# Every pair of f tiles goes by Strassen's scheme, with the sums of g's blocks made on GpSimd

## The chip, the cores and the metric

The kernel runs on one core of one Trainium2 chip. The metric is the device time of one execution in microseconds, and less is better. One core has five engines with instruction queues of their own: TensorE (PE in the profile, with its weight loads as PEld), VectorE (DVE), ScalarE (ACT), GpSimd (POOL) and SyncE (SP, which here issues transfers only). Each engine takes its instructions strictly in the order in which the program put them there, and waits on semaphores for the others.

## The reference

For each of 8 batches and 8 heads, 32 packed queries attend over 576 keys, and then the 576 queries attend over the 32 packed results. The heads are joined to a matrix of 4608 tokens by 512, and that goes through two matrix products with an ELU between.

```
def sm_attn(qq, kk, vv):
    a = softmax(scale * qq @ kk.T)          # with the maximum taken off, eps 1e-9
    return a @ vv
p_packed = sm_attn(p, k, v)                 # 8 x 8 x 32 x 64
x = sm_attn(q, p_packed, p_packed)          # 8 x 8 x 576 x 64 -> 4608 x 512
h = x @ w_in                                # 512 x 2048
g = where(h > 0, h, exp(min(h, 0)) - 1)
out = g @ w_out                             # 2048 x 512
```

## The kernel before, in words

**What is computed.** The first product is folded into the attention. `ppT` holds the packed results of a batch, `m` is `ppT` times `w_in` (the "m steps", line 838, four to a batch), and `h` is the second softmax `a` times `m`. Numbers are split into a rounded part and a remainder (`a_hi`, `a_lo`, `m_hi`, `m_lo`, and two parts of `g` and of the output weights `wo_a`, `wo_b`), so each product is three matmuls: high by high, high by low, low by high.

**Tiles.** The 2048 columns of `h` are 16 "f tiles" of 128. A batch's 576 tokens are two windows (`win` 0 and 1). One window has 256 tokens, the other 320, of which 64 are kept aside in `hb` and stored in DRAM (`rest_dram`); four batches' leftovers make a window of 256 at the end (`rest`, called batches 8 and 9 here). Batches 0, 1 and window (2, 0) go f tile by f tile (lines 1342 to 1455), with the weights still being converted on VectorE and ScalarE.

**Strassen's scheme.** From window (2, 1) on, f tiles go in pairs (`strassen_pair`, with `u` the pair's number, 8 pairs to a window). The 256 tokens by 256 columns of `g` are four blocks of 128 by 128, in a buffer `w8` (two of these; the leftovers' windows use a `kvq` buffer instead). For a Strassen pair three instructions (`sums`, line 1155) make four further blocks. ScalarE then casts seven blocks into `g` (`hi`), VectorE subtracts for the remainders (`lo`, line 1164), and TensorE makes seven products of three matmuls with 256 columns each: 21 matmuls on line 1229. The weights of these products are the stored blocks and four sums of them, `sw`, made once on VectorE (`strassen_weights`), written to DRAM (`sw_dram`), and fetched again for every Strassen pair: four loads of 256 KB (line 1187) into a ring of eight `sw` buffers. A pair that `S_PLAINS` names goes "plain" instead: no sums, four blocks in `hi` and `lo`, no `sw` loads, and either 12 matmuls of 512 columns (windows whose list has pair 0) or 6 of 512 and 12 of 256. `S_PLAINS` names 17 of the 88 pairs of batches 2 to 7.

**What sets the order.** Nothing is left to a runtime scheduler. The program collects operations with `op(prio, {engine: cost}, fn, deps, take, use, ...)`; `take` and `use` name buffers of rings (`R`: three `g`, two `w8`, eight `sw`, eight PSUM banks). `schedule()` then plays them through with these costs, `SWITCH` for every change of TensorE between full tiles and the small tiles (64 rows by 32 columns) of attention and m steps, lags and priorities, and writes each engine's queue in the order that comes out. The costs decide the order only; on the chip every wait is a semaphore.

**The ends.** At the start, `warm_up` runs `N_WARM` matmuls on a constant, and then TensorE follows batch 0's attention as its data comes. At the end, the last window and the second leftover window finish together (`both`); VectorE adds four accumulators in PSUM to `part` (`add1` to `add5`, line 1260), and SyncE stores two halves of it (line 1302).

Of the kernel before, what the change touches and what calls it, by code (L numbers as in the profile page):

```python
# [22 lines left out]
def packed_attention_elu_ffn(  # L23
# [63 lines left out]
    SPARE = 0.75  # L87
    HOLD = 2.1500000000000004
# [10 lines left out]
    SWITCH = 0.105  # L99
    N_WARM = 14  # L100
    F_PLAIN = 0
# [5 lines left out]
        (2, 0): [1, 2],  # L107
        (2, 1): [0],
        (3, 0): [1],
        (3, 1): [0, 2, 5],  # L110
        (4, 0): [0, 5],
        (4, 1): [1],
        (5, 0): [2, 7],
        (5, 1): [0, 4],
        (6, 0): [6],
        (6, 1): [1, 5, 6, 7],
# [38 lines left out]
    class Banks:  # L155
# [3 lines left out]
        def places(self, bufs, now):  # L159
            free = [h is None or h.released(now) for h in self.held]  # L160
            out = []
            for b in bufs:
                at = [i for i in range(0, len(free), b.n) if all(free[i:i + b.n])]
# [16 lines left out]
    class Buf:  # L180
        def __init__(self, ring, make, n=1):
            self.ring, self.make, self.n, self.users, self.t = ring, make, n, [], None
            self.free = False
# [7 lines left out]

    ops = []
# [3 lines left out]
    def op(prio, on, fn, deps=(), take=(), use=(), after=(), mode=None, lag=0):  # L196
        o = Op()
        o.lag = lag
# [8 lines left out]
    def schedule():  # L207
# [9 lines left out]
        idle_at = {e: 0.0 for e in GAP}  # L217
# [4 lines left out]
        def engine_for(o):  # L222
# [8 lines left out]
            e = min(o.on, key=lambda e: max(idle_at[e], now) + o.on[e] + spare * (e == "DVE"))  # L231
            return e if idle_at[e] <= now else None

        while todo:
            held = {}
            for n, o in enumerate(todo[:400]):
                if o.wait:
                    continue
                if o.ready > now:
                    if o.ready <= now + HOLD and o.prio < HOLD_K and len(o.on) == 1:  # L240
                        held.setdefault(*o.on, o)
                    continue
# [16 lines left out]
                idle_at[e] = now + cost + GAP[e]  # L259
                o.start, o.end = now, now + cost + LAG[e] + o.lag  # L260
# [94 lines left out]
    def warm_up(e):  # L355

        x = part_sb[:, 0, :E // 2].bitcast(BF16)
        for _ in range(N_WARM):
            nc.tensor.matmul(warm_b.t, lhsT=x[:, :P], rhs=x, start=True, stop=True)

    warm_b = banks(1)
    op(-1000, {"PE": 1.2 + 0.31 * N_WARM}, warm_up, take=[warm_b])
# [83 lines left out]
    def attention(b, ts):  # L446
# [182 lines left out]
        if b < S_FIRST[0] + 1:  # L629
            o1 = op(t, {"PE": 1.15}, s1, ld_k, take=ps1 + e1s, use=[p_b] + k_b, after=[free], mode=1)  # L630
# [6 lines left out]
        else:  # L637
            kept, o1 = [], None
            for half in range(2):
                ps = ps1[half]  # L640
                o1 = op(
                    t, {"PE": 0.52}, lambda e, half=half, ps=ps: s1_half(e, half, ps), ld_k,
# [56 lines left out]
        o = op(ts[2], {"PE": 1.36}, pv, ld_v + tr_done, take=[ps, pp_b], use=v_b + e1T, mode=2)  # L699
        done = []  # L700
        for g in range(G):
            def norm(e, g=g, ps=ps):
# [9 lines left out]
                ts[2], {"ACT": 0.31, "DVE": 0.27}, norm, [o, o5] + done,  # L712
# [15 lines left out]
        prev = []  # L728
        for half in range(2):
            ps = banks(2)  # L730
            t1, t2 = temp(), st.af if whole else temp()
# [12 lines left out]
            def fold(e, g, ps=ps, t1=t1):  # L744
                nc.vector.transpose(out=flat(t1)[:, g * HS:(g + 1) * HS], in_=ps.t[:, g, :HS])
# [46 lines left out]
            def lo(e, cs=cs, done=done):  # L792
# [6 lines left out]
            o = op(t, {"PE": 0.52}, s2, [lds["q"][half % len(q_b)], st.ppT_op],  # L799
                   take=[ps, t1], use=[q_b[half % len(q_b)], st.ppT], mode=1)  # L800
            f0 = op(t, {"DVE": 0.44}, lambda e, fold=fold: fold(e, 0), [o] + prev, use=[ps, t1])
            f1 = op(t, {"DVE": 0.44}, lambda e, fold=fold: fold(e, 1), [f0], use=[ps, t1])
# [21 lines left out]
    def mstep(b, c, part, parts_, prio, deps=()):  # L824
# [25 lines left out]
        def lo(e):  # L850
# [7 lines left out]
        if part:  # L858
            pre.append(st.m_done[c, part - 1])
        o = op(prio, {"PE": 1.0 / parts_ + 0.03}, mm, pre, take=[ps] + (m_b if part == 0 else []),  # L860
               use=[st.ppT] + (m_b if part else []), mode=1)
# [5 lines left out]
        if not whole:  # L867
            st.m_done[c, part] = op(
                prio, {"DVE": 1.2 if parts_ == 1 else 0.68}, lo, [h], use=[ps] + m_b
            )  # L870
        st.m_parts = parts_

# [46 lines left out]
    for b in range(B):  # L919
        for c in range(NFC):  # L920
# [3 lines left out]
            else:  # L924
                t = TMS[b] if b in TMS else TM
                mstep(b, c, 0, 1, first_use["b", b] - NS + t[c])
# [115 lines left out]
    def strassen_pair(i, b, win, f):  # L1042
# [103 lines left out]
        def sums(e):  # L1146
# [3 lines left out]
            for out, x, y, o in (  # L1150
# [3 lines left out]
            ):  # L1154
                nc.vector.tensor_tensor(out=out, in0=x, in1=y, op=o)  # L1155
# [17 lines left out]
        if not plain:  # L1173
            done = [op(i + 1, {"DVE": 1.08}, sums, done, use=[w8])]
# [26 lines left out]
        if f == 0:  # L1201
            accs[mine] = [banks(1) for _ in range(3)] + [accs["rest"][3] if both else banks(1)]
        acc = accs[mine]
# [49 lines left out]
        if last:  # L1253
# [38 lines left out]
            y = op(q, {"DVE": 0.69}, add4, [y, acc[2].last], use=[part, acc[2]])  # L1292
            y = op(q, {"DVE": 0.42 if both or rest else 0.69}, add5, [y, acc[3].last], use=[part, acc[3]])
# [6 lines left out]
            def store(e):  # L1300
                for r in range(2):
                    nc.sync.dma_start(
# [3 lines left out]
            op(q, {"DMA": 1.4}, store, [y], use=[part])  # L1306

    acc = None
    for i, (b, win, f) in enumerate(order):
# [119 lines left out]
        if first:  # L1429
            acc = [banks(1) for _ in range(n_t)]  # L1430

# [130 lines left out]
```

## Time and profile before

| what | value |
|---|---|
| median of 3 runs | 665.98 us (664.81 to 666.00) |
| the profiled execution | 665.54 us, of which 663.7 us are the span from first to last instruction |
| TensorE busy | 642.7 us (97%), 5963 matmuls |
| VectorE busy | 562.7 us (85%), 1270 instructions |
| ScalarE busy | 429.5 us (65%) |
| GpSimd busy | 19.4 us (3%), 27 instructions |
| moved from HBM | 124.25 MB read, 27.26 MB written |

Rows name a line of the kernel, an engine, an operation, and out<-in by the program's tile names. "Idle before" is time in which the engine had nothing running just ahead of these instructions, and behind it stands who ended that wait. Times inside the trace are in microseconds from the span's start. Matmuls overlap in the array, so their durations don't add up; what counts is the time from one's start to the next one's.

### The profile page before, as it was taken

To read this page: it belongs to the slowest core of one execution; us is meant where nothing else is said; L and a number is where in the kernel's file an instruction comes from. 1 tells how busy PE (TensorE), PEld (TensorE's weight loads), DVE (VectorE), ACT (ScalarE), POOL (GpSimd) and SP (SyncE) were. 2 spreads that over 40 slices of the span, in tenths; PEclk is the share of its full clock that TensorE was granted. 3 is DMA by queue.
4 is the path that set the end of the run, shared out by engine and by line. 5 is a ranking of instruction groups with operands and counts; after the bars stand their busy time and mean duration, and the time that the engine had idled before them with its cause. 6 is when DMAs were issued, how large, how long until landed. Compare 5 with 4: busy or idle time off the path is not lost.

```text
span 663.7 us, 15743 instructions
## 1 busy us (share of the span) xinstructions
PE 642.7 (97%) x5963; PEld 563.8 (85%) x5963; DVE 562.7 (85%) x1270; ACT 429.5 (65%) x863; POOL 19.4 (3%) x27
## 2 busy tenths in 40 slices
PE   6599999999999999999999999999999999999996
PEld 3277788898779898997889998998889988999996
DVE  2899889999995799978986998769999978878785
ACT  4599898777664567875575567675676566555451
POOL 0000101222110000000000000000000000000000
PEclk9699999999999999999999999999999999999999
DMA  8795973899951367888658887886589764785863
GB/s 339 297 316 173 298 244 80 202 211 263 320 195 27 116 215 247 261 260 265 231 173 290 289 253 243 283 259 235 163 283 319 240 199 123 222 229 186 284 227 132
DMA packets 94443, 152.55 MB, mean 230 GB/s; under 512 B 25248, under 2 KB 34464, under 8 KB 94112
## 3 DMA queue, kind: packets, MB, share of 16 engines
q1 hardware_dynamic: 91488, 146.30, 67.2%
q0 software_dynamic: 2880, 5.24, 5.3%
q8 instruction: 47, 0.77, 0.4%
q14 instruction: 28, 0.23, 0.1%
HBM read 124.25 MB, written 27.26 MB: 228 GB/s over the span
## 4 chain that ended last, share of the span: by engine, by line
PE 85%; ACT 6%; DMA 5%; DVE 2%; issue 1%; SPq 1%; POOL 0%; DVEq 0%; ACTq 0%; POOLq 0%
PE psum L1229 37%; PE psum L1073 20%; PE psum L1342 6%; PE psum L838 4%; PE psum L1452 4%; PE psum L1455 4%; PE psum L1453 4%; ACT tops L352 2%; DMA out<-part 2%; PE psum L737 1%; PE psum L692 1%; DMA raw<-in_w_out 1%; DMA kvq<-in_qT 1%; PE psum L596 1%; PE psum L666 1%
## 5 line engine op out<-in xcount | busy, mean ns | idle before, releaser
L1229 PE MATMUL psum<-sw,g 128*128 128x256 f32 x1044 | 150.4, 276 | 0.2 <-DMA sw<-sw_dram 0.2
L1229 PEld LDWEIGHTS psum<-sw,g 128*128 128x128 f32 x1044 | 133.0, 192 | 5.0 <-issue 3.5
L1164 DVE TENSOR_TENSOR g<-w,g 128x896 fp32r<-128x896 f32 (+1 forms) x88 | 88.4, 1006 | 21.1 <-ACT g L352 20.8
L1073 PE MATMUL psum<-a_hi,m_hi 128*128 128x320 f32 (+1 forms) x352 | 103.2, 293 | 0.1
L1073 PE MATMUL psum<-a_lo,m_hi 128*128 128x320 f32 (+1 forms) x352 | 101.4, 288 | 0.0
L1073 PE MATMUL psum<-a_hi,m_lo 128*128 128x320 f32 (+1 forms) x352 | 101.4, 288 | 0.0
L352 ACT CAST g<-w 128x896 fp32r<-128x896 f32 (+1 forms) x88 | 77.1, 876 | 35.6 <-PE psum L1229 16.3
L1229 PE MATMUL psum<-wo_a,g 128*128 128x256 f32 (+1 forms) x519 | 83.5, 293 | 0.0
L1229 PE MATMUL psum<-wo_b,g 128*128 128x256 f32 (+1 forms) x522 | 82.9, 290 | 0.0
L1229 PEld LDWEIGHTS psum<-wo_a,g 128*128 128x128 f32 x519 | 71.5, 191 | 5.2 <-issue 3.0
L1229 PEld LDWEIGHTS psum<-wo_b,g 128*128 128x128 f32 x522 | 70.8, 191 | 5.9 <-issue 3.5
L1155 DVE TENSOR_TENSOR w<-w 128x128 f32<-128x128 f32 (+1 forms) x213 | 70.8, 333 | 5.2
L1073 PEld LDWEIGHTS psum<-a_hi,m_hi 128*128 128x128 f32 x352 | 67.1, 191 | 7.5 <-issue 1.8
L1085 ACT ACTIVATE e<-psum 128x320 f32<-128x320 f32 x96 | 41.7, 434 | 40.4 <-PE psum L1073 37.0
L1073 PEld LDWEIGHTS psum<-a_lo,m_hi 128*128 128x128 f32 x352 | 67.2, 191 | 0.5
L1073 PEld LDWEIGHTS psum<-a_hi,m_lo 128*128 128x128 f32 x352 | 67.0, 190 | 0.0
L1085 ACT ACTIVATE w<-psum 128x512 f32<-128x512 f32 x40 | 23.8, 597 | 36.5 <-PE psum L1073 16.9
L1088 ACT ACTIVATE e<-e 128x320 f32<-128x320 f32 x96 | 45.1, 471 | 2.4
L1080 DVE SCALAR_TENSOR_TENSOR w<-e,psum 128x256 f32<-128x256 f32 x96 | 39.7, 414 | 8.1 <-ACT e L1088 7.9
L1360 ACT ACTIVATE e<-psum 128x256 f32<-128x256 f32 (+1 forms) x80 | 32.6, 407 | 21.5 <-PE psum L1342 17.4
L1369 DVE SCALAR_TENSOR_TENSOR e<-e,psum 128x256 f32<-128x256 f32 x80 | 33.0, 414 | 10.8 <-ACT e L1366 10.6
L838 PE MATMUL psum<-w_in_sb,ppT 64*32 64x512 f32 (+1 forms) x640 | 35.5, 518 | 6.0 <-DVE w_in_sb L397 5.8
(124 smaller groups left out, 1237.8 us busy)
## 6 DMA issues: line engine op xcount, KB each, us to landing
sw<-sw_dram SPq DMA_DIRECT2D x284, 256.0 KB, 3.9
kvq<-in_v SPq DMA_DIRECT2D x16, 512.0 KB, 5.4
out<-part SPq DMA_DIRECT2D x32, 256.0 KB, 3.6
sw_dram<-sw SPq DMA_DIRECT2D x32, 256.0 KB, 4.1
raw<-in_w_in SPq DMA_DIRECT2D x16, 511.8 KB, 4.5
raw<-in_w_out SPq DMA_DIRECT2D x16, 511.8 KB, 5.3
kvq<-in_kT SPq DMA_DIRECT2D x14, 576.0 KB, 5.1
kvq<-in_qT SPq DMA_DIRECT2D x14, 576.0 KB, 5.6
```

The lines of the kernel that those rows point to most:

```text
L352: (nc.scalar.copy if e == "ACT" else nc.vector.tensor_copy)(out=out, in_=in_)
L838: nc.tensor.matmul(ps.t[cols_of(pair), g, :w], lhsT=st.ppT.t[rows_of(g), pair, :], rhs=w_in_sb[rows_of(g), pair, c * FC + part * w:c * FC ...
L1073: nc.tensor.matmul(ps, lhsT=m_b[p].t[:, g, o:o + P], rhs=in_turn(st.a.t[q][:, g, cols]), start=(n == 0), stop=(n == 3 * G - 1),)
L1080: nc.vector.scalar_tensor_tensor(out=out, in0=e_, scalar=-1.0, in1=ps, op0=ALU.add, op1=ALU.max)
L1085: nc.scalar.activation(out=out, in_=ps, func=AF.Relu, scale=-1.0)
L1088: nc.scalar.activation(out=x, in_=x, func=AF.Exp, scale=-1.0)
L1155: nc.vector.tensor_tensor(out=out, in0=x, in1=y, op=o)
L1164: nc.vector.tensor_tensor(out=g_b.all[:, 7 * P:(7 + b1 - b0) * P], in0=blocks(b0, b1), in1=g_b.all[:, :(b1 - b0) * P].bitcast(F32), op=ALU ...
L1229: nc.tensor.matmul(a.t[:, at * H:(at + rhs.shape[1]) * H], lhsT=operand(blk, p), rhs=rhs, start=new and n == k == 0, stop=a.final == (u, m ...
L1342: nc.tensor.matmul(ps_b.t[:, :n_tok], lhsT=m_b[x].t[:, g, o:o + P], rhs=in_turn(st.a.t[y][:, g, cols]), start=(n == 0), stop=(n == 3 * G - 1),
L1360: nc.scalar.activation(out=pairs(e_b.t[:, :n_tok]), in_=h(slice(0, n_tok)), func=AF.Relu, scale=-1.0)
L1369: nc.vector.scalar_tensor_tensor(out=pairs(out), in0=pairs(e_b.t[:, cs]), scalar=-1.0, in1=h(cs), op0=ALU.add, op1=ALU.max,)
```

## The change

The three sums of a Strassen pair are issued to GpSimd in place of VectorE, as three operations with costs of their own, and `S_PLAINS` is empty, so all 88 pairs go by the scheme. The planner gets a resource "port": of the operations in `TWO`, one on VectorE and one on GpSimd are not placed at the same time. Several other costs and rules change with it: a higher `SWITCH`, m steps that follow each other in order, softmax folds of 2 x 288 columns in one VectorE instruction in place of two, banks limited for some accumulators, 20 fillers of two matmuls each at the start, and the last two stores placed apart. `M_PAIR`, `S1_FULL` and `S2_BOTH` are empty lists, so what hangs on them isn't reached.

```
-    SWITCH = 0.105
+    SWITCH = 0.2
     N_WARM = 14
+    N_FILL = 20
     S_PLAINS = {
-        (2, 1): [0],
...                               (17 pairs in all of windows (2, 1) to (6, 1), and 2 of (2, 0))
     }
+    TWO = {"top", "join", "high", "low", "ssub", "smul", "hi", "lo", "sub_own", "cast", "sums", "words", "t13", "t24"}
+            if o.two and e in ("DVE", "POOL") and idle_at["port"] > now:
+                return None
+    for _ in range(N_FILL):
+        warm_op = op(-30, {"PE": 0.44}, lambda e: warm_up(e, 2), after=[warm_op], use=[warm_b], lag=-0.2)
-            def fold(e, g, ps=ps, t1=t1):
-                nc.vector.transpose(out=flat(t1)[:, g * HS:(g + 1) * HS], in_=ps.t[:, g, :HS])
+            def fold(e, ps=ps, t1=t1):
+                nc.vector.transpose(
+                    out=flat(t1).rearrange("p (g s) -> p g s", g=G), in_=ps.t[:, :, :HS]
+                )
-        def sums(e):
+        def sums(e, at):
...
-                nc.vector.tensor_tensor(out=out, in0=x, in1=y, op=o)
+            nc.gpsimd.tensor_tensor(out=out, in0=x, in1=y, op=o)
-            done = [op(i + 1, {"DVE": 1.08}, sums, done, use=[w8])]
+            for n, cost in enumerate((0.41, 0.69, 0.41)):
+                done = [op(i + 1, {"POOL": cost}, lambda e, n=n: sums(e, n), done, use=[w8], lag=0.05 - LAG["POOL"], two=True)]
-            op(q, {"DMA": 1.4}, store, [y], use=[part])
+            if both:
+                op(q, {"DMA": 0.7}, lambda e: store(e, (1,)), [y4], use=[part])
+                op(q, {"DMA": 0.7}, lambda e: store(e, (0,)), [y], use=[part])
+            else:
+                op(q, {"DMA": 1.4}, store, [y], use=[part])
```

TensorE's queue at a pair that was plain, the third of window (3, 1), before (line 1073 is `h`, line 1229 the output products):

```order
L1073 MATMUL psum<-a_lo,m_hi 128x256
L1073 MATMUL psum<-a_hi,m_lo 128x256
L1229 MATMUL psum<-wo_a,g 128x512 x12
L1073 MATMUL psum<-a_hi,m_hi 128x256
L1073 MATMUL psum<-a_lo,m_hi 128x256
```

The same pair on TensorE after (line 1122 is `h`, 1281 the output products, 862 an m step):

```order
L1122 MATMUL psum<-a_lo,m_hi 128x256
L1122 MATMUL psum<-a_hi,m_lo 128x256
L1281 MATMUL psum<-wo_a,g 128x256 x3
L1281 MATMUL psum<-sw,g 128x256 x9
L1281 MATMUL psum<-wo_a,g 128x256 x6
L862 MATMUL psum<-w_in_sb,ppT 32x512 x8
L1281 MATMUL psum<-sw,g 128x256 x3
L1122 MATMUL psum<-a_hi,m_hi 128x256
```

Twelve matmuls of 512 columns became 21 of 256, twelve of which read `sw`. VectorE's queue in window (3, 0) before, where 1080 is the ELU's last step, 1155 the sums and 1164 the remainders (`w_3681` is a `w8` buffer):

```order
L1080 SCALAR_TENSOR_TENSOR w_3681<-e,psum 128x256
L1080 SCALAR_TENSOR_TENSOR hb<-e,psum 128x64
L1155 TENSOR_TENSOR w_3681<-w_3681 128x128
L1155 TENSOR_TENSOR w_3681<-w_3681 128x256
L1155 TENSOR_TENSOR w_3681<-w_3681 128x128
L1080 SCALAR_TENSOR_TENSOR w_3732<-e,psum 128x256
L1080 SCALAR_TENSOR_TENSOR hb<-e,psum 128x64
L1164 TENSOR_TENSOR g<-w_3681,g 128x896
```

VectorE's queue in that window after, with 1129 for the ELU and 1213 for the remainders:

```order
L1129 SCALAR_TENSOR_TENSOR w_3727<-e,psum 128x256
L1129 SCALAR_TENSOR_TENSOR hb<-e,psum 128x64
L1129 SCALAR_TENSOR_TENSOR w_3792<-e,psum 128x256
L1129 SCALAR_TENSOR_TENSOR hb<-e,psum 128x64
L1213 TENSOR_TENSOR g<-w_3727,g 128x896
```

The three sums are gone from between the ELU and the remainders; GpSimd's queue holds three of them for each pair instead, behind its 20 stores of the first batches. TensorE's queue at the start, after batch 0's product with `v`, before (718 and 737 are batch 0's second attention, 838 the first m step, 1335 the first `h`):

```order
L692 MATMUL psum<-kvq,tmp 32x64 x40
L718 MATMUL psum<-ident,pp 128x128
L737 MATMUL psum<-q_181,ppT 32x288 x16
L838 MATMUL psum<-w_in_sb,ppT 32x256 x8
L1335 MATMUL psum<-k_292,m_hi 128x256 x4
```

The same place after, where line 361 is a filler:

```order
L698 MATMUL psum<-kvq,tmp 32x64 x40
L361 LDWEIGHTS part
L361 MATMUL psum<-part 128x512
L361 LDWEIGHTS part
L361 MATMUL psum<-part 128x512
L724 MATMUL psum<-ident,pp 128x128
```

Fillers stand between the steps of batch 0's attention: 2 of the 40 matmuls ahead of its first product, 8 and 6 around its transposes, 2 here, 4 behind line 724 and 18 between the two halves of line 747, which was 737.

More of the change, by code (lines that the diff above doesn't have):

```diff
@@ L162, in places @@
             for b in bufs:
-                at = [i for i in range(0, len(free), b.n) if all(free[i:i + b.n])]
+                at = [i for i in range(0, min(len(free), b.lim), b.n) if all(free[i:i + b.n])]
                 if not at:
@@ L239, in schedule @@
                 if o.ready > now:
-                    if o.ready <= now + HOLD and o.prio < HOLD_K and len(o.on) == 1:
-                        held.setdefault(*o.on, o)
+                    if o.ready <= now + HOLD and o.prio < HOLD_K:
+                        for e in o.on:
+                            held.setdefault(e, o)
                     continue
@@ L259, in schedule @@
                 idle_at[e] = now + cost + GAP[e]
+                if o.two and e in ("DVE", "POOL"):
+                    idle_at["port"] = idle_at[e]
                 o.start, o.end = now, now + cost + LAG[e] + o.lag
@@ L727, in attention @@
         st.a_done, st.af_done = [], []
-        prev = []
+        prev, s2s = [], []
         for half in range(2):
-            ps = banks(2)
-            t1, t2 = temp(), st.af if whole else temp()
+            if half and b in S2_BOTH:
+                ps, t1 = second
+                t2 = temp()
+            else:
+                ps = banks(2)
+                t1, t2 = temp(), st.af if whole else temp()
             mx, sm = {}, {}
@@ L798, in attention @@
             t = ts[4 + half]
[L799 to L802, printed above, removed]
+            if b in S2_BOTH:
+                s2s.append((s2, ps, t1))
+                if half == 0:
+                    ps1_, t11 = banks(2), temp()
+                    second = ps1_, t11
+                    o2 = op(
+                        t, {"PE": 0.97}, lambda e: [x[0](e) for x in s2s], [lds["q"][0], lds["q"][1], st.ppT_op],
+                        take=[ps, ps1_, t1, t11], use=q_b + [st.ppT], mode=1,
+                    )
+                o = o2
+            else:
+                o = op(t, {"PE": 0.485}, s2, [lds["q"][half % len(q_b)], st.ppT_op],
+                       take=[ps, t1], use=[q_b[half % len(q_b)], st.ppT], mode=1)
+            f1 = op(t, {"DVE": 0.77}, fold, [o] + prev, use=[ps, t1])
             o = op(t, {"DVE": 0.75}, smax, [f1], use=[t1])
@@ L859, in mstep, with mstep_pair, mstep_done, done @@
             pre.append(st.m_done[c, part - 1])
-        o = op(prio, {"PE": 1.0 / parts_ + 0.03}, mm, pre, take=[ps] + (m_b if part == 0 else []),
-               use=[st.ppT] + (m_b if part else []), mode=1)
+        if also:
+            return ps, m_b, mm, pre, hi, lo_, whole
+        ready = mstep_done(b, c, part, parts_, prio, ps, m_b, hi, lo_, whole)
+        ready(op(prio, {"PE": 0.86 / parts_}, mm, pre, after=[b >= NB0 and m_last[0] or None],
+                 take=[ps] + (m_b if part == 0 else []), use=[st.ppT] + (m_b if part else []), mode=1))
+    def mstep_pair(b, c, prio):
+        st = sts[b]
+        both = [mstep(b, c + n, 0, 1, prio, also=True) for n in range(2)]
+        o = op(
+            prio, {"PE": 0.86 * 2}, lambda e: [x[2](e) for x in both], both[0][3] + both[1][3],
+            take=[x[0] for x in both] + both[0][1] + both[1][1], use=[st.ppT], after=[m_last[0]], mode=1,
+        )
+        for n, (ps, m_b, _, _, hi, lo_, whole) in enumerate(both):
+            mstep_done(b, c + n, 0, 1, prio, ps, m_b, hi, lo_, whole)(o)
+    def mstep_done(b, c, part, parts_, prio, ps, m_b, hi, lo_, whole):
+      st = sts[b]
+      def done(o):
+        m_last[0] = o
         h = op(
```

69 lines of the change are left out of this document (39 added, 30 removed).

## The prediction

> **What bounds the kernel now.** I read the page's totals and slices first, then TensorE's waits, then the chain that ended last. In these lines the slices show where TensorE is not full, and the chain which engine sets the end.
>
> ```profile
> span 663.7 us, 15743 instructions
> PE 642.7 (97%) x5963; PEld 563.8 (85%) x5963; DVE 562.7 (85%) x1270; ACT 429.5 (65%) x863; POOL 19.4 (3%) x27
> PE   6599999999999999999999999999999999999996
> PE 85%; ACT 6%; DMA 5%; DVE 2%; issue 1%; SPq 1%; POOL 0%; DVEq 0%; ACTq 0%; POOLq 0%
> ```
>
> TensorE is full but for the first slice and the last. Its waits say the same; each row has the total, how often, and the longest.
>
> ```profile
> PE psum L838 <- DVE w_in_sb L397: 5.8, 1, 5.8
> PE psum L666 <- ACT tmp L579: 2.9, 3, 2.1
> ...
> PE psum L1229 <- DMA sw<-sw_dram: 0.2, 1, 0.2
> ```
>
> The large ones lie in the first 37 us; the products of Strassen's scheme waited once, for 0.2 us. So VectorE at 85% is busy but in nobody's way, and taking sums from it gives nothing by itself. The time can only change by what TensorE has to stream, by waits that are new, and at the two ends. I make the sum against the profiled execution's 665.5 us, which lies 0.4 below the median of 665.98.
>
> **Plain pairs become Strassen pairs.** Here the chain has a plain pair (12 matmuls) and a Strassen pair (21) each in one piece; the other two rows count the 512-column matmuls that go.
>
> ```profile
> 318.88 2.59 PE psum L1229 x12
> ...
> 322.81 2.35 PE psum L1229 x21
> ...
> L1229 PE MATMUL psum<-wo_a,g 128*128 128x512 f32 x84 | 20.1, 381 | 0.0
> ...
> L1229 PE MATMUL psum<-wo_b,g 128*128 128x512 f32 x66 | 15.8, 381 | 0.0
> ```
>
> 2.59/12 is 0.216 us for 512 columns, 2.35/21 is 0.112 for 256. A plain pair of the first kind saves 2.59 - 2.35 = 0.24; of the second kind (6 wide, 12 narrow) 6 x 0.216 + 12 x 0.112 - 2.35 = 0.29. The 150 wide matmuls are 8 pairs of 12 and 9 of 6, so 8 x 0.24 + 9 x 0.29 = **-4.5 us**, all of it on the path.
>
> **Changes between full and small tiles.** TensorE's order after has 61 stretches of small tiles (attention, m steps) where it had 58. What a stretch costs beyond its columns:
>
> ```profile
> 262.47 0.83 PE L1229 MATMUL psum<-wo_b,g 128*128 128x256 f32 x6
> 263.23 1.09 PE L838 MATMUL psum<-w_in_sb,ppT 64*32 64x512 f32 x16
> 264.25 0.40 PE L1073 MATMUL psum<-a_hi,m_hi 128*128 128x320 f32 x1
> 264.49 0.30 PE L1073 MATMUL psum<-a_lo,m_hi 128*128 128x320 f32 x1
> ...
> 185.29 1.88 PE psum L838 x32
> ```
>
> Six narrow matmuls take 0.76 to the next start instead of 0.67 (0.09 going in); the first one behind takes 0.24, where the next of its kind takes 0.14 (0.10 coming out); one m step is 1.02 and two in a row 1.88, so 0.16 is paid once a stretch. Together 0.35, and three more are **+1.05 us**. The rest of TensorE's matmuls are the same in number and shape, fillers aside.
>
> **The start.** TensorE waited 5.8 us ahead of the first m step and then ran at a slow clock. Windows give engines' busy time, then the granted clock, DMA share and GB/s; then come TensorE's first products of `h`, and what VectorE waited for.
>
> ```profile
> 15.00:20.00 5.00, 2.12 (x33) 0.69 (x33) 3.12 (x7) 1.18 (x3) 0.00 (x0) 0.60 1.03 404
> 20.00:25.00 5.00, 1.11 (x16) 0.23 (x16) 4.86 (x10) 2.26 (x5) 0.00 (x0) 0.50 0.56 227
> 25.00:30.00 5.00, 4.85 (x32) 3.07 (x40) 3.23 (x7) 3.08 (x8) 0.00 (x0) 0.53 0.96 378
> ...
> 25.15 3.78 PE L1335 MATMUL psum<-k,m_hi 128*128 128x256 f32 x8 [0.74 <-ACT m_hi L352]
> 31.64 1.13 PE L1335 MATMUL psum<-k,m_hi 128*128 128x256 f32 x4 [0.77 <-ACT m_hi L352]
> ...
> 28.12 0.42 DVE L1369 SCALAR_TENSOR_TENSOR e<-e,psum 128x256 f32<-128x256 f32 x1 [0.97 <-ACT e L1366]
> 29.95 0.75 DVE L765 TENSOR_REDUCE sm<-tmp 128x18 f32<-128x576 f32 x1 [0.81 <-ACT tmp L761]
> ```
>
> At clock 0.5 eight rows took 3.78 us; at 1.00 four took 1.13, so eight would take about 2. The 18 fillers between the halves of line 737 occupy 18 x 0.216 = 3.9 of the 5.8 us that were idle, and should hold the clock. TensorE then finishes those products some 1.8 us sooner, but VectorE, behind ScalarE, can make up only the 0.97 + 0.81 = 1.8 us that it idled. Against it stand two fillers more ahead of batch 0's first product (0.4), of which I count half as late at the first m step. I take **-1.2 us**, between -1.8 (nothing late) and +0.4 (the clock falls anyway and the delay stays).
>
> **The end.**
>
> ```profile
> 658.61 1.34 DVE L1260 TENSOR_TENSOR part<-part,psum 128x256 f32<-128x256 f32 x3
> 659.98 0.84 SPq L1302 DMA_DIRECT2D out<-part  x2
> ```
>
> One of the last two stores now needs only `add4` and is issued during `add5`; the other's issue moves up by half of 0.84, **-0.4 us** (0 if both land together as before).
>
> **The sums on GpSimd.** They leave VectorE and add nothing to TensorE; their price is how much later `hi`, `lo` and the products come. The first two rows are the sums now, then `lo` of a Strassen pair and of a plain one, then all that GpSimd does here on 128 columns.
>
> ```profile
> L1155 DVE TENSOR_TENSOR w<-w 128x128 f32<-128x128 f32 x142 | 40.7, 286 | 2.8
> L1155 DVE TENSOR_TENSOR w<-w 128x256 f32<-128x256 f32 x71 | 30.2, 425 | 2.5
> ...
> L1164 DVE TENSOR_TENSOR g<-w,g 128x896 fp32r<-128x896 f32 x71 | 76.8, 1083 | 16.3 <-ACT g L352 16.1
> L1164 DVE TENSOR_TENSOR g<-w,g 128x512 fp32r<-128x512 f32 x17 | 11.6, 685 | 4.8 <-ACT g L352 4.7
> ...
> masks.py:199 POOL TENSOR_SCALAR_AFFINE_SELECT ident<-ident 128x128 f32<-128x128 f32 x1 | 0.3, 286 | 0.0
> masks.py:197 POOL MEMSET ident<- 128x128 f32 x1 | 0.2, 205 | 0.3 <-POOLq L1551 0.3
> ```
>
> On VectorE a pair's sums are 2 x 0.29 + 0.43 = 1.0 us. No row has a two-input instruction on GpSimd. From below: one input read and written took 286 ns, as on VectorE, so 1.0 again. From above: a write alone took 205; two reads and a write one after the other would be 0.6, and for three instructions with four blocks some 2.4. I take 1.5, nearer the row that reads and writes. So each pair's products are ready about 0.5 us later (0 to 1.4). The Trainium skill ("GPSIMD Engine Reference", "Performance versus the Vector engine") says an elementwise operation with two inputs takes GpSimd 1.96 times VectorE's time. By that estimate the sums are 2.0 us and the products 1.0 later; no run here shows it yet.
>
> What covers 0.5 us? The time between the end of `lo` and the first product that reads it, at a roomy pair and at a tight one:
>
> ```profile
> 591.32 1.09 DVE L1164 TENSOR_TENSOR g<-w,g 128x896 fp32r<-128x896 f32 x1 [0.62 <-ACT g L352]
> ...
> 597.29 0.50 PE L1229 MATMUL psum<-wo_b,g 128*128 128x256 f32 x3
> ...
> 623.65 1.09 DVE L1164 TENSOR_TENSOR g<-kvq,g 128x896 fp32r<-128x896 f32 x1 [1.05 <-ACT g L352]
> ...
> 625.09 0.50 PE L1229 MATMUL psum<-wo_a,g 128*128 128x256 f32 x3
> ```
>
> 4.9 us at the first, 0.35 at the second. Of 104 pairs about twenty have under 1 us, in (2, 1), (4, 1), the start of (5, 0) and the second leftover window. VectorE is lighter by 71 + 16 pairs x 1.0 = 87 us less 17 x 0.4 for longer `lo`, so its queue waits shrink in just these places, and the order puts 7 us and more of TensorE's work between `h` and its product nearly everywhere. Cover gone, each of twenty pairs could cost up to 0.5.
>
> **The loads of `sw`.** 17 pairs more are 68 loads. Windows of before; last two columns are the share of the DMA engines and GB/s:
>
> ```profile
> 305.00:495.00 190.00, 189.95 (x1950) 167.77 (x1940) 165.50 (x351) 119.20 (x218) 0.00 (x0) 1.00 0.76 246
> 305.00:347.00 42.00, 41.96 (x419) 34.21 (x409) 37.40 (x69) 26.14 (x45) 0.00 (x0) 1.00 0.67 219
> 456.00:495.00 39.00, 38.99 (x423) 33.64 (x422) 36.92 (x74) 25.49 (x44) 0.00 (x0) 1.00 0.65 216
> 494.00:519.00 25.00, 25.00 (x244) 23.05 (x229) 23.91 (x50) 14.91 (x26) 0.00 (x0) 1.00 0.91 309
> ```
>
> 309 GB/s at a share of 0.91 is 340 at 1, so a load of 256 KB is 0.77 us of all engines, a pair 3.1. Windows (3, 1) to (5, 1) get 10 pairs: 31 us on 190, and the share goes from 0.76 to about 0.93. A stretch at 0.91 ran without a wait of TensorE, so most is covered by the ring of eight buffers, with little to spare. On SyncE's queue a load that waits for its buffer holds the batch loads behind it. For both kinds of new waits I add **+1.4 us** (0 to 6).
>
> **Sum:** 665.5 - 4.5 + 1.05 - 1.2 - 0.4 + 1.4 = 661.9; with the median's 0.4 on top of the profiled time it would be 662.3. I predict **662.0 us**, own range 659 to 664.6.
>
> **Rivals.**
> - *The later sums eat the gain.* If GpSimd's sums are at 2.4 us, twenty tight pairs wait 0.5 to 0.7 longer than TensorE has work: 10 to 14 us less what a lighter VectorE gives back, which I put at two thirds. 662.3 less the 1.4 for waits is 660.9, and 4 more are about 665. For it: the tight row above. Against it: most pairs have 2 to 5 us.
> - *Transfers become the bound* (slower). If transfers can't hold a share over 0.88 for long, (3, 1) to (5, 1) need 190 x 0.93/0.88 = 201 us, 11 more on 660.9, about 672. It costs more than the gain once the share they can hold falls below 0.91. Against it: 0.91 over 25 us without a wait. For it: the stretch is now over 180 us long.
> - *The two engines exclude each other* (slower). If VectorE stands whenever GpSimd computes, the window at 305 needs 37.4 - 5 x 1.0 + 3 x 0.4 + 8 x 1.5 = 45.6 us of VectorE in 41.3, and the one at 456 needs 36.9 - 6.0 + 0.8 + 12 = 43.7 in 38.5; 4.3 + 5.2 more give about 670. GpSimd did nothing beside these windows before, so no row excludes it. It decides once about half of GpSimd's time is taken from VectorE. The rule behind it: the Trainium skill ("SBUF — State Buffer", "Who interferes with whom") has VectorE's instructions with two SBUF inputs and GpSimd's reads block each other for a whole instruction. Instructions with one input in PSUM don't count by that rule, which by it leaves the rows of `lo` and few others, and most of the price away.
> - *The start gives all and nothing waits:* 665.5 - 4.5 + 1.05 - 1.8 - 0.4 = 659.9, and 660.3 with the median's 0.4.
>
> That the change doesn't do what it says is excluded by GpSimd's queue, which has 312 sums for 104 pairs.
>
> **Chances.** My forecast 0.60; all covered 0.08; sums eat the gain 0.17; transfers 0.09; exclusion 0.06. 0.2% (1.3 us) is about what a measurement of this kernel can tell from no change. Faster by more (below 664.65): 0.60 + 0.08 + a little of the third, 0.70. Within: 0.16. Slower (over 667.3): the last two, less a little, 0.14. The range of 658.5 to 667.5 leaves the two slow cases out and some of the third.
>
> **What the profile after would show.** Line 1281 with 2184 matmuls at 0.112 us and none of 512 columns; TensorE's waits still without the sums' followers or `sw` above 1.5 us in total; clock 1.00 from 15 to 30 us and the first m step near 23.5; GpSimd's sums at about 0.4 and 0.7; DMA share near 0.93 from (3, 1) to (5, 1); VectorE near 73% (562.7 - 87 + 7 us). The prediction is wrong if line 1281 waits for `sw` or for the casts behind GpSimd by more than 5 us, or if VectorE's `lo` or ELU rows grow by tenths of a microsecond.

## The result: 1% slower, and TensorE waits where it did not

The changed kernel takes 671.6 us (670.73 to 672.4, 4 runs) where the kernel before, beside it on the same chip, takes 665.39 (664.21 to 666.0): a ratio of 1.0095, 95% interval 1.0082 to 1.0108. That is 6.2 us more, where 662.0 was predicted. Of one kernel below (sums on VectorE, tables fitted) the profiled execution ran at a granted clock of 0.75 and took 828 us, so it doesn't count there, and that row has no figure from a trace. The page of the changed kernel, in the lines that answer to those of before:

```profile
span 670.6 us, 16342 instructions
PE 648.8 (97%) x6102; PEld 566.1 (84%) x6102; DVE 505.4 (75%) x1006; ACT 429.4 (64%) x850; POOL 217.5 (32%) x339
PE   8799999999999999999999999998999999999996
PE 28%; DVE 9%; ACT 2%; POOL 2%; issue 1%; DMA 1%; DVEq 0%; ACTq 0%
```

VectorE fell from 85% to 75% and GpSimd rose from 3% to 32%, as meant. The chain that sets the end is no longer one long stretch of TensorE. TensorE's share of it fell from 85% to 28%, and the page can't follow it through all its links. The slices hide what happened: 97% and a row of nines look like before. A long window shows it. The columns are the window, then each engine's busy time and instructions, then granted clock, DMA share and GB/s. Before, and then after, for all of the work by Strassen's scheme but its last pairs:

```profile
200.00:655.00 455.00, 454.66 (x4320) 417.48 (x4320) 383.64 (x851) 276.76 (x501) 0.00 (x0) 1.00 0.71 225
```

```profile
200.00:655.00 455.00, 446.50 (x4359) 411.14 (x4358) 321.92 (x587) 275.39 (x488) 195.86 (x310) 1.00 0.82 262
```

TensorE stood still for 0.3 us of these 455 before, and for 8.5 us after. Its waits in that window after, with total, count and longest (before there was one, of 0.2 us, for `sw`):

```profile
PE psum L1281 <- DVE part L1312: 2.0, 2, 1.0
PE psum L1122 <- DVE w L1129: 1.5, 3, 0.9
PE psum L602 <- DVE m_lo L875: 1.5, 2, 1.3
PE psum L1281 <- ACT e L1137: 1.1, 1, 1.1
PE psum L1281 <- DVE w L1129: 0.7, 1, 0.7
PE psum L1122 <- DVE hb L1129: 0.6, 1, 0.6
PE psum L1122 <- DVE m_lo L875: 0.6, 2, 0.4
PE psum L1281 <- DVE hb L1129: 0.4, 1, 0.4
```

These add up to 8.4 us in thirteen places, and none is a wait for a transfer. By the releasers that the profile names they are waits for VectorE and ScalarE: for a PSUM bank that an ELU or an output add has to free, or for `m_lo`. So the gain of 4.5 us in columns was there, and nearly twice as much came back as small waits. The question for the experiments was whether GpSimd makes these waits, or the 17 new pairs, or the order in which the planner now puts the same work.

### The profile page after: what moved, and what is told of

The parts are those of the page before. It is cut to its first block, busy times and chain, and to the rows that moved or that the text cites. A ratio compares the mean times of both kernels' runs of the same rounds, so it can differ in the third digit from the quotient of the medians.

```text
span 670.6 us, 16342 instructions
## 1 busy us (share of the span) xinstructions
PE 648.8 (97%) x6102; PEld 566.1 (84%) x6102; DVE 505.4 (75%) x1006; ACT 429.4 (64%) x850; POOL 217.5 (32%) x339
## 5 line engine op out<-in xcount | busy, mean ns | idle before, releaser
L1204 POOL TENSOR_TENSOR w<-w 128x128 f32<-128x128 f32 (+1 forms) x264 | 167.4, 636 | 250.2 <-DVE w L1129 215.1
L1281 PE MATMUL psum<-sw,g 128*128 128x256 f32 x1248 | 182.4, 277 | 0.7 <-DVE w L1129 0.7
L1281 PEld LDWEIGHTS psum<-sw,g 128*128 128x128 f32 x1248 | 159.9, 192 | 10.7 <-issue 7.8
L1213 DVE TENSOR_TENSOR g<-w,g 128x896 fp32r<-128x896 f32 x88 | 101.6, 1154 | 63.1 <-ACT g L354 60.6
L354 ACT CAST g<-w 128x896 fp32r<-128x896 f32 x88 | 82.6, 938 | 63.8 <-POOL w L1204 54.4
L1558 POOL DMA_DIRECT2D out<-part x20 | 17.8, 1002 | 178.5 <-ACT part L354 149.0
L1281 PE MATMUL psum<-wo_a,g 128*128 128x256 f32 x468 | 70.4, 277 | 3.6 <-DVE part L1312 2.0
L1281 PE MATMUL psum<-wo_b,g 128*128 128x256 f32 x468 | 70.1, 277 | 0.0
L1281 PEld LDWEIGHTS psum<-wo_a,g 128*128 128x128 f32 x468 | 60.9, 192 | 8.6 <-issue 2.5
L875 DVE TENSOR_TENSOR m_lo<-psum,m_hi 128x1024 fp32r<-128x1024 f32 (+1 forms) x36 | 37.2, 1039 | 5.8 <-ACT m_hi L354 5.6
```

Of the source, the lines that this page charges most:

```text
L354: (nc.scalar.copy if e == "ACT" else nc.vector.tensor_copy)(out=out, in_=in_)
L875: nc.vector.tensor_tensor(out=m_b[1].t[:, :, fs], in0=ps.t[:, :, :w], in1=m_b[0].t[:, :, fs].bitcast(F32), op=ALU.subtract,)
L1204: nc.gpsimd.tensor_tensor(out=out, in0=x, in1=y, op=o)
L1213: nc.vector.tensor_tensor(out=g_b.all[:, 7 * P:(7 + b1 - b0) * P], in0=blocks(b0, b1), in1=g_b.all[:, :(b1 - b0) * P].bitcast(F32), op=ALU ...
L1281: nc.tensor.matmul(a.t[:, at * H:(at + rhs.shape[1]) * H], lhsT=operand(blk, p), rhs=rhs, start=new and n == k == 0, stop=a.final == (u, m ...
L1558: nc.gpsimd.dma_start(out=out[r0:r1, :], in_=part.t, accum_op=ALU.add)
```

## The experiments

The theories, as the expectations name them: **A**, the sums end late on GpSimd and `hi` and `lo` stand for them, with all that is queued behind; **B**, VectorE and GpSimd stand for each other; **C** and later **O**, the order has the waits, whoever does the sums, because the planner's tables of due times fit the old costs; **D**, the loads of the new pairs; **L**, the rule that keeps accumulators in four PSUM banks; **G**, GpSimd or the 17 pairs, whatever the mechanism. Ratios are to the kernel before on the same chip.

| kernel | median us | ratio (95% interval) | TensorE not busy, 200 to 655 us |
|---|---|---|---|
| after | 671.6 | 1.0095 (1.0082 to 1.0108) | 8.5 us |
| sums back on VectorE | 677.42 | 1.0188 (1.0175 to 1.0202) | 11.9 |
| nothing waits for the sums | 668.69 | 1.0058 (1.0046 to 1.0070) | 6.7 |
| and the sums cut to 8 columns | 668.31 | 1.0057 (1.0044 to 1.0069) | 6.1 |
| plain pairs put back | 676.16 | 1.0177 (1.0156 to 1.0198) | 6.9 |
| new planner, old work | 678.66 | 1.0203 (1.0188 to 1.0218) | 10.0 |
| before, fold in one instruction | 677.18 | 1.0189 (1.0171 to 1.0207) | 5.6 |
| new work, old planner | 679.59 | 1.0224 (1.0203 to 1.0245) | 11.0 |
| after without fillers | 674.64 | 1.0148 (1.0125 to 1.0171) | 8.9 |
| after, tables fitted | 665.70 | 1.0007 (0.9999 to 1.0016) | 3.5 |
| sums on VectorE, tables fitted | 668.40 | 1.0049 (1.0034 to 1.0063) | |
| fitted, nothing waits for the sums | 664.85 | 1.0001 (0.9991 to 1.0011) | 3.2 |
| second fit | 666.65 | 1.0019 (1.0010 to 1.0029) | 3.5 |

The last column has idle time alone. In four of these kernels (plain pairs put back; new planner, old work; before with the fold in one instruction; after without fillers) the traces show something more behind a wait: the granted clock falls to 0.5 for 3.4 us, twice in the second and the third of them. By estimate each such stretch costs 1.7 us. After has none between 29 us and its last matmul.

**The sums back on VectorE.**

```
-            for n, cost in enumerate((0.41, 0.69, 0.41)):
-                done = [op(i + 1, {"POOL": cost}, lambda e, n=n: sums(e, n), done, ...)]
+            done = [op(i + 1, {"DVE": 1.08}, lambda e: [sums(e, n) for n in range(3)], done, ...)]
```

> The changed kernel with the three sums back on VectorE as one operation with a cost of 1.08 (planned anew); every pair by the scheme, fillers and the planner's other rules as after. Theory A (the sums on GpSimd end later than planned and `hi` on ScalarE and `lo` on VectorE stand for them, with all that is queued behind): about 664, since the 8.4 us of new stalls of TensorE beyond 50 us go and VectorE is back near 86% busy. Theory B (VectorE and GpSimd stand for each other): 664 too. Theory C (the order that the planner's new rules and costs make has the stalls, whoever does the sums): 669 to 672. Theory D (17 pairs more of loads): 669 to 672, with TensorE waiting for sw.

It got 5.8 us worse, not better: 677.42, and no theory had that (664, or 669 to 672). The order is a new one too, so this doesn't price GpSimd. The window and the largest wait:

```profile
200.00:655.00 455.00, 443.11 (x4313) 405.85 (x4312) 393.98 (x878) 279.74 (x496) 0.00 (x0) 1.00 0.81 260
```

```profile
PE psum L1280 <- DVE part L1311: 5.4, 7, 2.4
```

Products wait for the adds that free the last window's accumulators, and these adds stand in VectorE's queue. With 72 us more on VectorE there are seven such waits in place of two. So waits of this kind come without GpSimd as well, and A and B can't be the whole cause of them; what they are worth in the order of after, the next two runs tell.

**Nothing waits for the sums, order kept.** `hi` and `lo` read block 1 seven times in place of blocks 1 to 7; every queue is that of the changed kernel.

```
-            copy(e, g_b.all[:, :(b1 - b0) * P], blocks(b0, b1))
+            copy(e, g_b.all[:, :7 * P].rearrange(...), blocks(1).unsqueeze(1).to_broadcast([P, 7, P]))
```

> The changed kernel with its order kept instruction for instruction and GpSimd's sums at full size, but `hi` and `lo` read block 1 seven times in place of blocks 1 to 7, so nothing waits for the sums (the output is not the reference's). Theory A: the waits of ScalarE for GpSimd (54 us) go, and TensorE's new stalls with them: about 664. Theory B: the sums still run beside VectorE and both still stand for each other, so lo stays near 1.15 us and the sums near 0.56 and 0.78: about 669 to 671. Theories C and D: 670 to 672.

668.69, between A's 664 and the 670 to 672 of C and D, and just under B's range: 2.9 us less than after by the medians, 2.5 by the ratios (0.0037 of 665), and the two intervals don't touch. ScalarE's row for `hi` shows that the wait is gone; the first row is after, the second this kernel:

```profile
L354 ACT CAST g<-w 128x896 fp32r<-128x896 f32 x88 | 82.6, 938 | 63.8 <-POOL w L1204 54.4
```

```profile
L354 ACT CAST g<-w 128x896 fp32r<-128x896 f32 x88 | 82.3, 935 | 21.1 <-PE psum L1285 20.6 <-DVE w L1129 0.5
```

54 us of waiting on ScalarE were worth 2.5 to 2.9 us at the end. That is the most that late sums can have cost: in the windows of 320 tokens block 1 comes from the first of two ELU instructions, so here `hi` doesn't wait for the second one either. The other 6.7 us in which TensorE stands still stay, at the same places.

**The sums cut to 8 columns as well, order kept.**

```
-            nc.gpsimd.tensor_tensor(out=out, in0=x, in1=y, op=o)
+            nc.gpsimd.tensor_tensor(out=out[..., :8], in0=x[..., :8], in1=y[..., :8], op=o)
```

> As the one in which nothing waits for the sums, and each sum is cut to 8 columns of every block, so GpSimd has next to nothing to do; the order on every engine is that of the changed kernel (the output is not the reference's). Theory A: as without the wait, about 664. Theory B: lo back at 1.09 and the stalls gone, 662 to 664, and several us below the kernel in which nothing waits. Theories C and D: 670 to 672, since order and loads are the same.

668.31, which no theory had, and a ratio of 1.0057 against 1.0058: taking GpSimd's work away beside VectorE changes nothing that can be measured, though `lo` is back at its old time:

```profile
L1216 DVE TENSOR_TENSOR g<-w,g 128x896 fp32r<-128x896 f32 x88 | 95.8, 1088 | 42.8 <-ACT g L354 42.4
```

So the two engines do stand for each other (below), but with nothing waiting for the sums the price at the end is about 1 us at most (each interval is 0.8 us to either side); that the sums themselves get longer beside VectorE is part of the 2.5 us. What is left, some 6 us of waits of TensorE, is not GpSimd's work. The order is the suspect, and the runs from here on test it.

**The plain pairs put back**, sums of the others on GpSimd.

```
     S_PLAINS = {
+        (2, 0): [1, 2], (2, 1): [0], (3, 0): [1], ...      (as before)
     }
```

> The changed kernel with the 17 plain pairs of before put back in S_PLAINS (planned anew), sums of the others on GpSimd. Theories A and B: 4.5 us of columns come back and 17 of 104 pairs lose their sums, so about 8.4 x 17/104 = 1.4 of stalls go: 674 to 675. Theory C: 675 with the same stalls, or anything between 668 and 678 if the order alone decides. Theory D: the loads are as before, so the stalls go: about 667.

676.16, by the ratios 5.5 us over after, with intervals of 0.9 and 1.4 us to either side. It fits the 4.5 us of columns, though the order is a new one too (its trace has a wait of 2.6 us near 469 us, and behind it a granted clock of 0.5 from 472.0 to 475.4 us), so this run doesn't prove the figure. D, which wanted 667, is out: the trace of after also has no wait of TensorE for `sw`.

**The new planner with the old work**, and **one edit to before that only the planner can mind**:

```
             (the changed kernel with the sums on VectorE, and)
+        (2, 1): [0], (3, 0): [1], ...        (S_PLAINS of before)
```

> The changed kernel's planner, fillers, fold and split stores, but the sums on VectorE (one operation, cost 1.08) and the 17 plain pairs of before: only what the change did to the order is left of it. Theory O (the tables of due times belong to the old costs, and every edit that the planner sees gives another order with stalls of its own): 672 to 682. Theory G (the loss came from GpSimd or from the 17 pairs): 664 to 666, as before.

```
-            f0 = op(t, {"DVE": 0.44}, lambda e, fold=fold: fold(e, 0), [o] + prev, use=[ps, t1])
-            f1 = op(t, {"DVE": 0.44}, lambda e, fold=fold: fold(e, 1), [f0], use=[ps, t1])
+            f1 = op(t, {"DVE": 0.77}, fold, [o] + prev, use=[ps, t1])
```

> The kernel before with one edit: the softmax fold is one VectorE instruction of 2 x 288 columns (cost 0.77) in place of two (0.44 each), which takes 0.1 us of VectorE's time a fold away and adds nothing. Theory O: the planner makes another order, with about as many columns on TensorE and new stalls: 671 to 678. The rival, that only work counts: 664.5 to 665, since VectorE is not the bound.

678.66 and 677.18: O holds in both, and G and the rival are out. The second one is the clearest run of this study. It does the same work in fewer VectorE instructions, and it is 12.3 us slower, since the planner answered with another order. One place holds nearly all of it: counted in the two traces, the 1861st of all output products starts at 555.92 us where it started at 555.46, and the 1981st at 587.55 where it started at 575.50. The window in this kernel, the same window before, and then what VectorE did in this kernel while TensorE waited:

```profile
560.00:582.00 22.00, 17.23 (x101) 15.32 (x100) 16.51 (x42) 10.45 (x19) 0.00 (x0) 0.84 0.33 105
```

```profile
560.00:582.00 22.00, 22.00 (x188) 21.95 (x187) 18.42 (x45) 11.96 (x21) 0.00 (x0) 1.00 0.65 191
```

```profile
562.63 0.76 DVE L776 TENSOR_TENSOR tmp<-tmp,sm 128x576 f32<-128x576 f32 x1
563.43 0.78 DVE L789 STREAM_TRANSPOSE tmp<-tmp 128x576 f32<-128x576 f32 x1
564.24 0.46 DVE L352 CAST a_hi<-tmp 128x576 fp32r<-128x576 f32 x1
...
564.75 0.40 PE L1074 MATMUL psum<-a_hi,m_hi 128*128 128x320 f32 x1 [1.71 <-DVE a_hi L352]
```

The last batch's second softmax came so late in VectorE's queue that TensorE had nothing left to stream; with the gaps the granted clock fell to 0.84, and 101 matmuls ran in 22 us where 188 had. The sums are on VectorE here, so GpSimd has no part in it.

**The new work with the old planner:**

```
     SWITCH = 0.105, costs, fold, stores and start as before; no port rule
+    S_PLAINS = {}; sums on GpSimd (0.41, 0.69, 0.41)
+    m steps in their order (after=[m_last[0]]); a.lim = 8 if both else 4
```

> The kernel before with the sums on GpSimd and no plain pair, planned with before's costs and SWITCH 0.105, without port rule, fillers, fold or split stores; of the new rules only the order of the m steps and the limit of four banks for accumulators, without which the old planner finds no order. Theory O: 660 to 668, since this order has fewer stalls by its own account. Theory L (the limit on the accumulators' banks makes the stalls at window starts): 670 to 673, with TensorE waiting about 1 us for the part adds at each window start. Theory A (late sums): about 3 us over an order without stalls, 663 to 665.

679.59, a miss for O, which had trusted the old planner's own reckoning and said 660 to 668, and for A (663 to 665). Its order has 11.0 us of standing still. L's 670 to 673 is missed as well, but 4.7 us of its waits are for the part adds. So the length that this planner reckons with the old costs was no guide here. The same work took 671.6 us in one order and 679.59 in another, so GpSimd with all pairs by the scheme is not good or bad in itself.

**Without the fillers**, all else in the same order:

```
-    N_FILL = 20
+    N_FILL = 0
```

> The changed kernel without the 20 fillers; all other instructions in the same order on every engine. By the prediction's step the fillers bring 1.2 us (with -0.4 to 1.8 as bounds): 672.8 (671.2 to 673.4). Rival: the clock at the start is no faster with them, and TensorE's idle time there is not what the end waits for: 671.6, within 0.5.

674.64 against 671.6, above the bounds of the expectation; the intervals leave 1 to 6 us. Part of that comes later: a wait of 1.8 us for a load from `in_qT` near 174 us (0.3 in after) and, behind it, a clock of 0.5 from 177.1 to 180.6 us. At the 81st matmul of line 1511 (134 us) the traces stand at 135.20 without and 134.16 with fillers, so I put them at 1.0 us. Windows of after at the start, and the first products of `h`:

```profile
15.00:20.00 5.00, 5.00 (x37) 2.08 (x38) 3.44 (x6) 1.29 (x4) 0.00 (x0) 1.00 1.03 403
20.00:25.00 5.00, 2.18 (x37) 0.63 (x35) 4.86 (x9) 2.70 (x5) 0.00 (x0) 1.00 0.66 239
25.00:30.00 5.00, 5.00 (x56) 2.78 (x56) 4.09 (x8) 3.29 (x8) 0.00 (x0) 0.66 0.91 328
```

```profile
24.83 3.09 PE L1392 MATMUL psum<-k,m_hi 128*128 128x256 f32 x8 [0.74 <-ACT m_hi L354]
```

**The tables fitted anew.** Same operations and rules; `T_ATTS`, `TMS`, `T_SE` and the other lead times come from a search over this planner's plans, with the sums at the cost that the trace showed.

```
-        3: [-2.5, 3.5, 12.0, -91.0, 4.0, 29.5],
+        3: [-3.0, -97.0, -45.0, -10.0, -14.0, 36.5],
...                               (T_ATTS and TMS of batches 3 to 7, T_ATT, T_ATT1, TM, ...)
-            for n, cost in enumerate((0.41, 0.69, 0.41)):
+            for n, cost in enumerate((0.46, 0.74, 0.46)):
```

> The changed kernel with the same operations and rules, sums planned at what the trace showed of them undisturbed (0.46, 0.74, 0.46), and its tables of due times and lead times (T_ATTS, TMS, T_SE and others) fitted anew by a search for the shortest plan of this planner. Theory O (the old tables are what makes the stalls): of the 9.9 us in which TensorE is not busy between 50 and 655 us at least 6 go, 661 to 666. Theory A or B (late sums, VectorE and GpSimd in each other's way) as the main cause: the stalls stay with the engines, 668 to 671. Theory L (the four banks): the waits for the part adds stay, 667 to 670.

665.70, as O had it: 5.9 us of the 6.2 are back by numbers that the planner alone reads. The window, and TensorE's waits in it:

```profile
200.00:655.00 455.00, 451.50 (x4425) 416.86 (x4424) 324.26 (x579) 278.01 (x501) 204.19 (x312) 1.00 0.83 264
```

```profile
PE psum L1122 <- DVE hb L1129: 1.7, 2, 1.1
PE psum L602 <- DVE mx L611: 0.8, 1, 0.8
PE psum L1122 <- DVE part L1312: 0.3, 1, 0.3
PE psum L1281 <- ACT tmp L629: 0.2, 1, 0.2
PE psum L672 <- DVE m_lo L875: 0.2, 1, 0.2
```

The four-bank rule still holds in this kernel, and the waits for the part adds are down from 2.0 to 0.3 us: L on its own is out as the cause. It leaves this kernel level with before, not ahead: from 50 to 200 us the fitted order waits 3.7 us where after waits 1.1.

The same with the sums on VectorE, and tables fitted for that:

```
+            done = [op(i + 1, {"DVE": 1.08}, lambda e: [sums(e, n) for n in range(3)], done, ...)]
...                               (T_ATTS, TMS and the lead times: other numbers)
```

> As the fitted one, but with the sums on VectorE (one operation of 1.08) and tables fitted for that. If taking 104 us of sums from VectorE is worth something once the order suits: 3 to 8 us over the fitted kernel with GpSimd, 666 to 672. If VectorE's load doesn't matter, as the prediction had it (busy but in nobody's way): within 1 us of the fitted kernel, or below it by the 2 to 3 us that late sums cost.

668.40, a ratio of 1.0049 against 1.0007: with an order fitted for each, the kernel with sums on GpSimd is 2.8 us ahead, a little under the 3 to 8 of the expectation. Each order comes from a search of its own, and nothing shows that the two fit equally well, so this is not a price of the engine.

And the fitted kernel, order kept, with the edit that lets nothing wait for the sums:

```
+                blocks(1).unsqueeze(1).to_broadcast([P, 7, P]),       (for blocks(1, 8), in hi and lo)
```

> The fitted kernel with its order kept, where hi and lo read block 1 seven times, so nothing waits for GpSimd's sums (the output is not the reference's). In the changed kernel that was worth 2.9 us. If late sums hurt because the order left them no cover: 0 to 1 us under the fitted kernel. If they hurt in any order: 2 to 4 us under it.

664.85, 1.0001 against 1.0007; the intervals overlap. Late sums cost up to 2.5 us in the order of after and nothing measurable here, though ScalarE's `hi` still waits 33.1 us for them in the fitted kernel.

**A second fit**, with the tables of the first batches left alone, so as to keep what after has there:

```
-        3: [-2.5, 3.5, 12.0, -91.0, 4.0, 29.5],
+        3: [21.5, -7.0, -15.5, -60.0, 8.5, 36.0],
...                               (T_ATTS, TMS and the lead times; T_ATT, T_ATT1, TM, LM, LOOK as after)
```

> A second fit of the tables of the changed kernel, in which those of the first batches (T_ATT, T_ATT1, TM, LM, LOOK) stay as they are, since the first fit won nothing there: in its trace TensorE waited 3.7 us between 50 and 200 us, in the changed kernel 1.1. Theory O: waits of TensorE of 3 to 5 us from 200 to 655 us, about 1 before, and 662 to 665. If fitted tables can't be better than before whatever they are: 665 to 667.

666.65, a miss for O; the other reading, no better than before, had 665 to 667. TensorE stands still for 3.5 us from 200 to 655 us as in the first fit, and the start of the scheme's work upsets the end of the first batches all the same (it waits 2.6 us from 50 to 200). No version that I ran beats before. Whether a better fit would reach the 662 of the prediction stays open; nothing that was measured forbids it, and nothing shows it.

## Why the prediction was wrong, step by step

- *Plain pairs, -4.5 us: right.* Line 1281 has 1248 + 468 + 468 = 2184 matmuls, all of 256 columns, at a pitch of 0.112 us (16.43 us for 147 in a row at the end):

```profile
L1281 PE MATMUL psum<-sw,g 128*128 128x256 f32 x1248 | 182.4, 277 | 0.7 <-DVE w L1129 0.7
L1281 PE MATMUL psum<-wo_a,g 128*128 128x256 f32 x468 | 70.4, 277 | 3.6 <-DVE part L1312 2.0 <-ACT e L1137 1.1 <-DVE hb L1129 0.4
L1281 PE MATMUL psum<-wo_b,g 128*128 128x256 f32 x468 | 70.1, 277 | 0.0
```

- *Changes between tiles, +1.05: too high.* Counted in the traces, small-tile stretches beyond 50 us hold 57.2 us of TensorE where they held 55.3. But 2.6 us of that are waits inside the stretches, 0.7 before, so all of the 1.9 is waiting, which belongs to the last step. What the changes themselves cost, going in and coming out included, came to about +0.5.
- *The start, -1.2: right in sign, too high.* By the 81st matmul of line 1452 (1511 after) after is 0.7 us ahead of before (134.16 against 134.88). The fillers kept TensorE full until 20 us, but did not reach up to the first m step at 23.4: TensorE was busy for 2.18 of the next 5 us, the clock was 0.66 in the 5 us behind that, and the eight products took 3.09 us, not the 2 that I had taken. So "should hold the clock" failed.
- *The end, -0.4: wrong.* From the start of TensorE's last matmul to the end of the span it is 5.99 us, before 5.75. Both stores of `part` are issued 0.3 us earlier, but the last DMA packet ends 4.38 us behind that start, before 4.39.
- *The loads: right.* From 305 to 495 us the DMA share is 0.91 (0.93 predicted), and no product waited for `sw`:

```profile
305.00:495.00 190.00, 186.19 (x2037) 167.80 (x2026) 145.49 (x257) 120.29 (x211) 74.07 (x123) 1.00 0.91 303
```

- *The sums, 1.5 us a pair: close.* Left alone (window 385 to 420) they take 2 x 0.459 + 0.733 = 1.65. Over the whole run the means are higher, 1.91 a pair:

```profile
L1204 POOL TENSOR_TENSOR w<-w 128x128 f32<-128x128 f32 x14 | 6.4, 459 | 23.2 <-DVE w L1129 22.7
L1204 POOL TENSOR_TENSOR w<-w 128x256 f32<-128x256 f32 x7 | 5.1, 733 | 0.5
...
L1204 POOL TENSOR_TENSOR w<-w 128x128 f32<-128x128 f32 x176 | 98.9, 564 | 243.8 <-DVE w L1129 215.1 <-DVE sm L780 13.7 <-DVE nb L621 8.3
L1204 POOL TENSOR_TENSOR w<-w 128x256 f32<-128x256 f32 x88 | 68.7, 781 | 6.4
```

- *Waits, +1.4 (0 to 6): the step that failed.* They were 8.4 us. The term had looked for them at products that stand for the casts behind GpSimd's sums, or for `sw`, and none of the thirteen is of that kind: they are for banks and for `m_lo`. The cover that it had counted held: from the end of `lo` to the pair's first product 15 of 104 pairs have under 1 us, where 13 had before (the prediction said about twenty). Even the part that late sums made shows at `h`: of the rows above, the one with three waits of `h` for an ELU (1.5 us) is gone where nothing waits for the sums.

Two sentences in front of this term were wrong. "The order puts 7 us and more of TensorE's work between `h` and its product nearly everywhere" counts the matmuls that lie between two others, and not when VectorE's queue gets to what they need. And "its queue waits shrink in just these places" took VectorE's queue to be as before with the sums taken out, where the planner had dealt all of it anew. One of the two waits for an output add shows how this looks. The chain of waits, and VectorE's queue ahead of it:

```profile
382.59 1.00 DVE g L1213
383.59 0.34 DVE part L1312
383.93 0.04 issue
383.98 2.87 PE psum L1281 x21
```

```profile
380.45 0.41 DVE L1312 TENSOR_TENSOR part<-part,psum 128x256 f32<-128x256 f32 x1
380.78 1.21 DVE L875 TENSOR_TENSOR m_lo<-psum,m_hi 128x1024 fp32r<-128x1024 f32 x1
381.92 0.67 DVE L1312 TENSOR_TENSOR part<-part,psum 128x512 f32<-128x512 f32 x1
382.51 1.08 DVE L1213 TENSOR_TENSOR g<-w,g 128x896 fp32r<-128x896 f32 x1
383.52 0.41 DVE L1312 TENSOR_TENSOR part<-part,psum 128x256 f32<-128x256 f32 x1
```

Window (4, 1) opens here. Its first product needs a bank that `add3` frees, and VectorE has an `m_lo` and a `lo` between the adds. VectorE is 75% busy over the run and has not a gap for 4 us here.

- *"Taking sums from it gives nothing by itself"* is in doubt, and not settled. In two pairs of kernels, one with old tables and one with fitted ones, the kernel with the sums on VectorE is slower, by 5.8 and by 2.8 us, but in each pair the order differs too. What is shown is that VectorE, in nobody's way at 85% in the order of before, is in TensorE's way at 75% in the order of after.
- *The sum.* With the sizes found, -4.5 + 0.5 - 0.7 + 0.2 + 8.4 is 3.9 of the 6.2 us. Part of the rest is that a wait costs more than its idle time: a matmul of 256 columns lasts 0.277 us in the rows, while the next one would start after 0.112, so 0.165 us of each wait are hidden. For thirteen waits that is an estimated 2 us.
- *The signs of being wrong* did not show: line 1281 waits 4.3 us in all and never for `sw` or for the casts behind GpSimd, and `lo` grew by 0.07 us, not by tenths. They watched the engines of the change, and the waits were at other places.
- *The rivals.* Later sums do cost, up to 2.5 of the 4 us that this rival had. Transfers did not bind. Exclusion is real and costs about 1 us at most. The rival that happened was not among them: that the plan itself is the worse one. It was to be had from the diff, which changes a dozen costs and rules of the planner and not one number of the tables of due times. What it costs was not to be had from there.

## What to carry to other kernels

Where a planner with fitted tables writes the queues, an edit is two changes: the work, and the order. Here the columns were worth what their rows said (4.5 us), and each of the six kernels whose order came from the old tables after an edit was 6 to 15 us slower than before, even where the edit only merged two instructions. So predict the order's share apart and with a wide range, and fit the tables again before judging the edit. For the waits look at TensorE's idle time in a long window and at its list of waits, since the page's 97% is the same for 0.3 us and for 8.5.

## What the runs showed of the hardware that I had not expected

GpSimd's small sums cost less against VectorE than I had feared: 459 against 286 ns on 128 columns and 733 against 425 on 256, ratios of 1.6 and 1.7, where the Trainium skill ("GPSIMD Engine Reference", "Performance versus the Vector engine") measured 1.96 on 2048.

A sum on GpSimd and a VectorE instruction with two inputs in SBUF kept each other out for whole instructions. Here are VectorE's `lo` and GpSimd's sum of 128 columns, which alone take 1.09 and 0.46 us, side by side:

```profile
301.28 1.16 DVE L1213 TENSOR_TENSOR g<-w,g 128x896 fp32r<-128x896 f32 x1 [1.15 <-ACT g L354]
...
301.57 1.18 POOL L1204 TENSOR_TENSOR w<-w 128x128 f32<-128x128 f32 x1
```

The sum was issued 0.29 us into `lo` and ended 0.31 us after it. Of the 312 sums some 40 were stretched like this, to between 0.71 and 1.63 us, always beside a VectorE instruction with two inputs in SBUF (`lo`, `a_lo`, or the softmax's subtraction and scaling); beside ELU, part adds and `m_lo`, which read PSUM, they kept 0.46 and 0.73. That is the rule of the Trainium skill ("SBUF — State Buffer", "Who interferes with whom"), and the trace agrees with it to the instruction. Where the sum came first, `lo` was the longer one: up to 1.65 us beside a sum of 256 columns that kept its 0.73, and 1.15 in the mean. With nothing waiting for the sums, all this was worth about 1 us at most.

The granted clock fell behind short gaps, but not behind each. After 2.8 us without work from 20 to 25 us it was 0.66 over the next 5 us; with the gaps of the kernel with the merged fold it was 0.84 over 22 us; after one wait of 1.8 us near 174 us the kernel without fillers ran at 0.50 from 177.2 to 180.5 us. But a wait of 2.4 us near 384 us left it at 1.00 until 400 us in the kernel with the sums back on VectorE, and the waits of up to 1.3 us in the order of after never moved it. What decides between them, these runs don't show.
